# Twelve of 36 weight chunks of the second MoE decoded during the last attention block, in slots that attention no longer uses

## The chip, the cores and the metric

One core of one Trainium2 chip runs the whole program: attention, a first mixture-of-experts layer (MoE) and a second one, in float32 inputs and outputs. The metric is the device time of one execution in microseconds (us), here the median of 3 runs. A core has five engines that work side by side, each through its own instructions in order: TensorE (PE, matmuls; PEld is its weight load), VectorE (DVE), ScalarE (ACT), GpSimd (POOL) and SyncE (SP, which here issues nearly all transfers). They wait for each other by semaphores.

## The reference

```python
def _attn_ref(q, k, v, w1, b1, w2):              # q, k, v: (4, 8, 576, 64)
    scores = scale * np.matmul(q, k.transpose(0, 1, 3, 2))
    ...
    h = np.maximum(x @ w1 + b1, 0.0)             # x: relative positions
    bias = h @ w2
    scores = scores + bias.transpose(2, 0, 1)[None, :, :, :]
    scores = scores - np.max(scores, axis=-1, keepdims=True)
    attn = np.exp(scores)
    attn = attn / (np.sum(attn, axis=-1, keepdims=True) + 1e-09)
    return np.matmul(attn, v).astype(np.float32)

def _moe_ref(x, w_in, w_out, g_ln):              # x: (2304, 512), w_in: (512, 1024)
    h = x @ w_in
    ...
    solu = h * sm                                # sm: softmax of h
    ln = (solu - mu) / np.sqrt(var + 1e-06) * g_ln
    return (ln @ w_out).astype(np.float32)

def _moe2_ref(x, w_gate, w_val, w_out):          # w_gate, w_val: (512, 1536), w_out: (1536, 512)
    gate = 1.0 / (1.0 + np.exp(-(x @ w_gate)))
    val = x @ w_val
    return (gate * val @ w_out).astype(np.float32)
```

The three follow each other: the second MoE reads what the first one wrote for the same tokens.

## The kernel before

**Arithmetic.** Matmuls take float16. Each float32 operand is scaled by a power of two and split into a high and a low float16 half, and a product is three matmuls (high x high, high x low, low x high). The MoE weights come in as 64-bit words, loaded as two 32-bit integers per value.

**A chunk.** A weight chunk is 128 rows by 512 values. The second MoE has 36: 12 each of gate, value and output weights, in column groups jc = 0, 1, 2 of four chunks. Each goes through the same steps:

1. load (L660): SP issues a 512 KB transfer into a raw tile `wraw`;
2. decode (L166 to L176): one step on ScalarE (L171) and three on VectorE (L172, L173, L176) make float32 of the integers, in place in `w2f`;
3. the square's sum on ScalarE (L1087), for the scale;
4. the scale of a column group (`w2_scale`), from sums on TensorE (L147, L1097) and a chain of small VectorE steps; for the output weights one scale for all (`w2_scale_out`, the last of the four; its end is L1112);
5. split (L663 to L669): GpSimd scales (L665), ScalarE writes the high half (L668), GpSimd the low half (L669), again in place.

**Attention.** It runs in 72 ticks, one per (batch pair, query block, head pair, ...). Tick t does the score matmuls (L530), the maximum with the bias added on VectorE (L550), the exponentials on ScalarE (L557); a step later the split of the probabilities (L568 on ScalarE or L566 on VectorE, L569 and L570 on GpSimd) and a transposing transfer by SP (L572); four steps later the PV matmuls (L590). The loop runs steps 0 to 77. K, V and bias live in 24 slots of one tile `gk`: 16 for the K and V of a batch pair by head pair, 8 for biases in rotation. The last block (batches 2 and 3, second query block) is ticks 56 to 71. Its head pairs leave their K and V one after the other, the last PV being that of tick 71.

**The first MoE** fills the gaps: its 18 token tiles are cut into pieces (`moe_items`), of which up to three are issued per step. A tile goes: first product on TensorE (L737), maximum (L748), exponential, normalization and square on VectorE and ScalarE (L756 to L768), scaling on GpSimd (L770, L771: the e step), transposes (L780), halves (L782, L783), second product (L794), and the store of the result x2 by SP (L802). Five or so tiles are left when attention ends.

**The second MoE's weights** are worked on from then on. All pieces stand in one list, `units`: 36 decodes, 3 + 1 scales, 36 splits. `W2A` = 12 are issued when attention is over (L1133), `W2B` = 10 behind each further x2 store (L1139: nothing of them is issued ahead of that store on the issuing engine), the rest among the gate and value products of the first token group (`gate_val`, L1304, with VectorE's steps L1310 and L1172, a pair per 128 columns). Three raw tiles rotate. Behind `w2_scale_out` VectorE forms sums and differences of weight blocks (`w2_sums`, 98 additions with those of the tokens, all at L1190), with which the token groups from the third on are computed by seven products in place of eight (`product`, L1266). The second product of the layer is `second_out` (L1334, 36 matmuls per tile).

**What sets the order.** TensorE follows the program's order inside the attention loop. Elsewhere, and on the other engines, a scheduler orders the instructions by priorities and modelled times; once ordered, every engine works strictly in order, and SP's transfers too.

Line numbers here and in the prediction are those of the kernel before.

Of the kernel before, what the change touches and what calls it, by code (L numbers as in the profile page):

```python
# [91 lines left out]
def attn_moe_kernel(  # L92
# [996 lines left out]
    def w2_split(mat, jc, c):
        split_w(w2f[mat][:, 4 * jc + c], sw[:, jc, S_G + mat:S_G + mat + 1], w2h16[mat][:, 4 * jc + c, 0],  # L1090
                w2h16[mat][:, 4 * jc + c, 1], w2t_p.tile([128, 512], F32, name="w2tmp", tag="w2sgn"))

    def w2_scale(jc):
        pow2(w2st, [(4 * jc, 4 * jc + 4)], sw[:, jc, P_G:P_G + 1], sw[:, jc, S_G:S_G + 1], psx[0], 13)
        tot = (psx[0] or ps_v).tile([128, 512], F32, name="cols", tag="m" if psx[0] else "v")
        for c in range(4):
            pe.matmul(tot, ones16, w2h.pop(("sq", jc, c)), start=(c == 0), stop=(c == 3))  # L1097
        mx = sm0.tile([128, 1], F32, name="colmax", tag="colmax")
        dve.tensor_reduce(out=mx, in_=tot, axis=AX, op=ALU.max)
        root2(mx, 1, sw[:, jc, P_L:P_L + 1], sw[:, jc, S_L:S_L + 1], 13)  # L1100
        dve.scalar_tensor_tensor(out=sw[:, jc, W_CG:W_CG + 1], in0=col(P_F), scalar=2.0 ** -21,
                                 in1=sw[:, jc, P_G:P_G + 1], op0=ALU.mult, op1=ALU.mult)

# [350 lines left out]
```

## Time and profile before

| | us |
|---|---|
| median of 3 runs (lowest, highest) | 1081.53 (1080.61, 1082.23) |
| the profiled execution: its own time | 1084.97 |
| its span, first to last instruction | 1083.2 |
| PE busy (share) | 910.7 (84%) |
| DVE busy (share) | 768.5 (71%) |
| ACT busy (share) | 619.4 (57%) |
| POOL busy (share) | 413.0 (38%) |

The profile is of one execution, and all times in the trace are counted from the start of its span. "Busy" of TensorE is not a pace: matmuls overlap, and their ends are modelled. So its pace is read from a run of like matmuls that follow each other. "Idle before" says how long an engine waited ahead of an instruction and who released it.

### The profile page before, as it was taken

How to read it: one execution, taken by the hardware profiler on the slowest of the kernel's cores; microseconds unless marked ns; L12 is line 12 of the kernel's file. 1: busy time of each engine (PE TensorE's matmuls, PEld its weight loads, DVE VectorE, ACT ScalarE, POOL GpSimd, SP SyncE). 2: the span in 40 equal slices, each digit the busy share in tenths (PEclk: the TensorE clock that was granted, in tenths of full speed). 3: DMA queues.
4: the chain of work that ended last, by engine and by line, in shares of the span. 5: the costliest groups of instructions: out<-in, count | busy, mean ns of one | idle time of the engine just before them, and what ended most of it. 6: DMA issues, size and time to landing. Idle time of an engine off the chain costs nothing. (4 is left out here: it accounts for less than half of the span.)

```text
span 1083.2 us, 24445 instructions
## 1 busy us (share of the span) xinstructions
PE 910.7 (84%) x9806; PEld 652.1 (60%) x9806; DVE 768.5 (71%) x1552; ACT 619.4 (57%) x1283; POOL 413.0 (38%) x370
## 2 busy tenths in 40 slices
PE   2556573768887889989999888896999999999998
PEld 2534453555666667676776656344577866865873
DVE  6879997985566676655755899999973862881760
ACT  4787775767676788776973777744342331331331
POOL 2366555745556555544560377758000000000000
PEclk9756665868999889989999898898999999999999
DMA  7979999899799799998965556501001010001001
GB/s 229 289 240 205 238 229 275 157 232 204 158 191 192 165 200 191 190 211 169 172 124 159 162 156 181 170 20 39 30 18 52 1 55 24 2 1 39 2 1 39
DMA packets 261442, 146.58 MB, mean 135 GB/s; under 512 B 217680, under 2 KB 231504, under 8 KB 261328
## 3 DMA queue, kind: packets, MB, share of 16 engines
q1 hardware_dynamic: 259264, 143.18, 56.2%
q0 software_dynamic: 1536, 1.58, 0.5%
q8 instruction: 77, 1.26, 0.5%
q10 hardware_dynamic: 528, 0.26, 0.1%
q14 instruction: 37, 0.30, 0.1%
HBM read 82.46 MB, written 20.05 MB: 95 GB/s over the span
## 5 line engine op out<-in xcount | busy, mean ns | idle before, releaser
L569 POOL TENSOR_TENSOR p<-p,p 128x1024 f16<-128x1024 f32 x72 | 154.7, 2149 | 150.1 <-ACT p L568 112.9
L1190 DVE TENSOR_TENSOR fr<-prod,fr 128x512 f32<-128x512 f32 x126 | 85.2, 688 | 93.8 <-PE prod L1266 92.1
L1334 PE MATMUL ops<-w2f,gv 128*128 128x512 f16 x648 | 144.2, 381 | 5.3 <-POOL w2f L669 3.9
L794 PE MATMUL x2ps<-lt,w1f 128*128 128x128 f16 x1728 | 114.0, 228 | 18.2 <-DVE lt L783 13.4
L557 ACT ACTIVATE p<-p,m,sc 128x576 f32<-128x576 f32 x144 | 124.0, 862 | 2.7
L794 PEld LDWEIGHTS <-w1f 128*128 128x128 f16 x1728 | 107.6, 103 | 28.6 <-issue 21.1
L550 DVE CUSTOM_DVE_ANT_0 p<-s_ps,gk 128x576 f32<-128x576 f32 x144 | 104.3, 751 | 21.9 <-PE s_ps L530 19.0
L1334 PEld LDWEIGHTS <-gv 128*128 128x128 f16 x648 | 63.6, 98 | 80.6 <-issue 7.4
L1304 PE MATMUL s_ps<-xb,w2f 128*128 128x512 f16 (+1 forms) x576 | 100.1, 332 | 8.8 <-DVE fr L1310 8.5
L590 PE MATMUL xps<-gk,pt 128*128 128x64 f16 (+1 forms) x2240 | 89.2, 203 | 17.8 <-DMA pt<-p 14.9
L590 PEld LDWEIGHTS <-pt 128*128 128x128 f16 (+1 forms) x2240 | 82.9, 107 | 29.1 <-DMA pt<-p 19.1
L530 PE MATMUL s_ps<-gk,qt 64*128 64x288 f16 (+1 forms) x960 | 91.9, 316 | 6.3 <-DVE m L550 3.7
L443 PEld LDWEIGHTS <-mask 128*128 128x128 f16 (+1 forms) x1312 | 60.9, 116 | 58.2 <-issue 24.3
L1266 PEld LDWEIGHTS <-w2f 128*128 128x128 f16 x864 | 84.5, 98 | 11.8 <-issue 1.1
L1304 PEld LDWEIGHTS <-w2f 128*128 128x128 f16 x576 | 56.9, 100 | 50.2 <-issue 14.5
L1171 ACT ACTIVATE gv<-fr 128x512 f16<-128x512 f32 (+1 forms) x60 | 34.7, 584 | 83.5 <-DVE fr L1324 70.5
L737 PE MATMUL hps<-w1f,xt 128*128 128x512 f16 x312 | 76.6, 396 | 0.6 <-DVE qt L282 0.6
L443 PE MATMUL bp<-rhs,mask 128*128 128x64 f16 (+1 forms) x960 | 52.2, 221 | 25.8 <-DVE gb L463 14.6
L555 ACT ACTIVATE m<-m,sc 128x1 f32<-128x1 f32 x144 | 40.6, 286 | 58.0 <-DVE m L550 58.0
L1266 PEld LDWEIGHTS <-w2s 128*128 128x128 f16 x648 | 63.4, 98 | 7.3
L568 ACT ACTIVATE p<-p 128x1152 f16<-128x1152 f32 x54 | 62.6, 1159 | 5.4 <-DMA pt<-p 3.8
L737 PEld LDWEIGHTS <-xt 128*128 128x128 f16 x384 | 36.9, 101 | 46.8 <-issue 12.1
(192 smaller groups left out, 1776.2 us busy)
## 6 DMA issues: line engine op xcount, KB each, us to landing
gk<-bias_d SPq DMA_DIRECT2D x24, 576.0 KB
wraw<-in_moe_w_out_dram SPq DMA_DIRECT2D x20, 512.0 KB
wraw<-in_moe_w_gate_dram SPq DMA_DIRECT2D x12, 512.0 KB
wraw<-in_moe_w_val_dram SPq DMA_DIRECT2D x12, 512.0 KB
sraw<-in_q_dram SPq DMA_DIRECT2D x12, 384.0 KB
sraw<-in_k_dram SPq DMA_DIRECT2D x12, 384.0 KB
sraw<-in_v_dram SPq DMA_DIRECT2D x12, 384.0 KB
bias_d<-gk SPq DMA_DIRECT2D x8, 576.0 KB
```

The source lines that it names most:

```text
L443: pe.matmul(big[0:np_, jj // 8, o:o + 64], lhsT, rhs[i].rearrange("p c h g -> p (c h g)"), start=(i == 0), stop=(i == 1),)
L530: glob["qk"] = pe.matmul(ss[hh][p0:p1, n, 0:288], qt[rows, nr * ql + r, p0:p1], kt[rows, o:o + 288], start=(m == 0), stop=(m == 2))
L550: dve.tensor_tensor_reduce(out=pp[:, hh].rearrange("p (i j) -> p i j", i=2), in0=ss[hh][:, :, 0:288], in1=bi.rearrange("p (i j) -> p i j", ...
L557: act.activation(out=pp[:, hh], in_=pp[:, hh], func=ACTF.Exp, bias=m[:, 2 + hh:3 + hh], scale=col(C), accum_out=sm[:, c + hh:c + hh + 1])
L569: pool.tensor_tensor(out=p16[:, :, 640:1152], in0=pp[:, :, 0:512], in1=hi[:, :, 0:512], op=ALU.subtract)
L590: pe.matmul(o, a, b_, start=(n == 0), stop=(n == len(seq) - 1))
L737: pe.matmul(h, xt[:, xl, kk, off:off + 128], win16[:, 2 * kk + n, wl], start=(kk == 0 and xl == 0 and wl == 0), stop=(kk == 3 and xl == 1),)
L794: pe.matmul(ps[:, dc], wout16[:, f, wl, 128 * dc:128 * dc + 128], lt[:, ll, f], start=(n == 0), stop=(n == 23))
L1190: dve.tensor_tensor(out=out_, in0=a, in1=b, op=op)
L1266: pe.matmul(p[:, jf, 0:nn], w(wl, kk, jf), x(xl, kk), start=(m == 0), stop=(m == 5))
L1304: pe.matmul(ps[:, 0:n], w[:, 4 * (j // 4) + c, wl, o:o + 128], xx[:, 0:n, c, xl, :], start=(m == 0), stop=(m == 11))
L1334: pe.matmul(ps, gvs[j // 4][:, gl, j % 4, 128 * tt:128 * tt + 128], w2h16[2][:, j, wl], start=(m == 0), stop=(m == 35))
```

## The change

Twelve of the 36 decodes move into the last attention block and its end. `AHEAD` lists for each the step of its load, the step of its decode, and the place of the raw words: 0 and 1 are two tiles of a new pool, 8, 10, 12 and 14 are bias slots of `gk` that are no longer read. The load is issued behind the transpose of the tick before (`tc.issue_after`), the decode behind the latest conversion of probabilities on ScalarE (`glob["hi"]`), both without the priority that attention's own work has. The decoded words no longer have tiles of their own (`w2f`): gate and value chunks and six of the output chunks go into `gk` (`gk32`, the same tile in rows of 512), where K, V and biases were, the other six into `w2x`. The squares of the first value chunks go into the raw K and V tile. When attention is over, 29 of the 76 pieces have been issued with `W2A` = 16, in place of 12; the thirteenth piece, the first group's scale, stands at attention's end.

```diff
@@ -47,7 +47,9 @@
+AHEAD = ((60, 63, 0), (61, 64, 1), (65, 67, 0), (66, 68, 1), (67, 69, 8), (69, 71, 10), (70, 72, 0), (70, 73, 1),
+         (71, 74, 8), (72, 75, 10), (73, 76, 12), (74, 76, 14))
-W2A = 12
+W2A = 16
...
+    kvr = kraw_p.tile([128, NKR, 2, 5, D], F32, name="kv")
+    kvraw = [kvr[:, i] for i in range(NKR)]
...
+    W2AT = ((20, 0, 10), (24, 4, 14), (8, 9, 18, 19, 28, 29))
+
+    def w2(mat, j, n=1):
+        if mat == 2:
+            t, a = (gk32, W2AT[2][j]) if j < 6 else (pools["w2x"], j - 6)
+        else:
+            t, a = gk32, W2AT[mat][j // 4] + j % 4
+        return t[:, a] if n == 1 else t[:, a:a + n]
...
+    def w2_early(n, t):
+        mat, jc, c = W2SEQ[n]
+        place = AHEAD[n][2]
+        if place < 2:
+            raw = pools["w2r"].tile([128, 512, 2], I32, name="wraw", tag=f"wraw{place}")
+        else:
+            raw = gk[0][:, place:place + 2].rearrange("p s e -> p (s e)")[:, 0:1024].bitcast(I32) \
+                .rearrange("p (f t) -> p f t", t=2)
+        src, rows, cols = w2_src(mat, jc, c)
+        with tc.issue_after(trs[min(t, nticks) - 1].ins):
+            sp.dma_start(out=raw.rearrange("p f t -> p (f t)"), in_=src[rows, cols].bitcast(I32))
+        early[mat, jc, c] = raw
+
+    def w2_dec(mat, jc, c):
+        raw = early.pop((mat, jc, c), None)
+        if raw is None:
+            raw = load_w(pools["w2r"], *w2_src(mat, jc, c))
+        w = w2(mat, 4 * jc + c)
+        decode(w, raw, pool if c < W2P else dve)
...
@@ -1052,7 +1152,20 @@
                 a_pv(t - LAG_PV)
             if 0 <= t - LAG_PV - LAG_X < nticks:
                 a_xt(t - LAG_PV - LAG_X)
+        if t == AHEAD[0][0]:
+            ahead = ExitStack()
+            pools["w2r"] = enter(ahead, "w2e", 1)
+        for n, (t0, t1, _) in enumerate(AHEAD):
+            if t == t1:
+                with tc.issue_after(glob["hi"].ins):
+                    units.pop(0)()
+        for n, (t0, t1, _) in enumerate(AHEAD):
+            if t == t0:
+                w2_early(n, t)
     in_order.close()
+    while len(units) > 76 - 13:
+        units.pop(0)()
+    ahead.close()
     att.close()
...
-    w2r_p = enter(d2, "w2r", 3, "right")
-    w2d_p = enter(d2, "w2d", 1, "right")
-    w2f = [w2_p.tile([128, 12, 512], F32, name=f"w2f{i}") for i in range(3)]
+    pools["w2r"] = enter(d2, "w2r", 3, "right")
+    pools["w2d"] = enter(d2, "w2d", 1, "right")
+    pools["w2x"] = w2_p.tile([128, 6, 512], F32, name="w2x")
```

How the order changes is seen in three places. On SP, from the last transposes of attention on, the order before is this (x_d is the store of x2, xb its load for the second MoE, wraw a chunk's raw words):

```order
L572 DMA_TRANSPOSE pt<-p_9418 128x18x128
L572 DMA_TRANSPOSE pt<-p_9527 128x18x128
L802 DMA x_d<-x_9581 128x1024
L572 DMA_TRANSPOSE pt<-p_9620 128x18x128
L1153 DMA xb<-x_d 128x4x1024
L802 DMA x_d<-x_9870 128x1024
L660 DMA wraw<-in_moe_w_gate_dram 128x1024 x4
L660 DMA wraw<-in_moe_w_val_dram 128x1024 x4
L660 DMA wraw<-in_moe_w_gate_dram 128x1024
```

After the change, whose early loads are at its line 1062 and whose other lines are up to two further down than before, from the same transposes on:

```order
L574 DMA_TRANSPOSE pt<-p_9571 128x18x128
L804 DMA x_d<-x_9625 128x1024
L1062 DMA gk<-in_moe_w_gate_dram 128x1024
L574 DMA_TRANSPOSE pt<-p_9670 128x18x128
L1062 DMA gk<-in_moe_w_gate_dram 128x1024 x3
L1205 DMA xb<-x_d 128x4x1024
L804 DMA x_d<-x_9938 128x1024
L662 DMA wraw<-in_moe_w_val_dram 128x1024 x4
L662 DMA wraw<-in_moe_w_gate_dram 128x1024 x4
L804 DMA x_d<-x_10315 128x1024
L662 DMA wraw<-in_moe_w_val_dram 128x1024
L804 DMA x_d<-x_10541 128x1024
```

Eight more loads of this kind stand ahead of these rows, between the transposes; behind the last row come the fifteen loads that are left. On ScalarE, around the conversion of tick 66 (the x2 tiles are x, the chunk's words gk or wraw), the order before is:

```order
L557 ACTIVATE p,sums<-p,m,sc 128x576 x2
L568 ACTIVATE p_9100<-p 128x2x576
L767 ACTIVATE hs,mm<-e,mm 128x1024
L555 ACTIVATE m<-m,sc 128x1
L557 ACTIVATE p,sums<-p,m,sc 128x576
L555 ACTIVATE m<-m,sc 128x1
L281 ACTIVATE qt<-qtp,sc 128x256
L557 ACTIVATE p,sums<-p,m,sc 128x576
```

And after it (L173 is the decode's step, L1077 the square's sum, L559 the exponential, L570 the conversion):

```order
L559 ACTIVATE p,sums<-p,m,sc 128x576 x2
L570 ACTIVATE p_9123<-p 128x2x576
L173 ACTIVATE gk<-wraw 128x512
L769 ACTIVATE hs,mm<-e,mm 128x1024
L557 ACTIVATE m<-m,sc 128x1
L559 ACTIVATE p,sums<-p,m,sc 128x576
L283 ACTIVATE qt<-qtp,sc 128x256
L557 ACTIVATE m<-m,sc 128x1
L559 ACTIVATE p,sums<-p,m,sc 128x576
L1077 ACTIVATE kv,w2st<-gk 128x512
```

The third decode's first step stands directly behind the conversion of tick 66, ahead of tick 67's exponentials, and its square's sum behind them. On GpSimd, when attention's last split is done, the order before has three e steps (mm, e) between the last probabilities and the first split of a chunk:

```order
L570 TENSOR_TENSOR p_9620<-p,p_9620 128x2x64
L770 TENSOR_TENSOR mm<-mm,nhalf 128x1
L771 TENSOR_SCALAR e<-e,mm 128x1024
L770 TENSOR_TENSOR mm<-mm,nhalf 128x1
L771 TENSOR_SCALAR e<-e,mm 128x1024
L770 TENSOR_TENSOR mm<-mm,nhalf 128x1
L771 TENSOR_SCALAR e<-e,mm 128x1024
L665 TENSOR_SCALAR w2tmp<-w2f_9972,sw 128x512 x2
```

After it:

```order
L572 TENSOR_TENSOR p_9670<-p,p_9670 128x2x64
L772 TENSOR_TENSOR mm<-mm,nhalf 128x1
L773 TENSOR_SCALAR e<-e,mm 128x1024
L667 TENSOR_SCALAR w2tmp<-gk,sw 128x512 x2
L671 TENSOR_TENSOR gk<-w2tmp,gk 128x512 x2
L667 TENSOR_SCALAR w2tmp<-gk,sw 128x512 x2
L671 TENSOR_TENSOR gk<-w2tmp,gk 128x512 x2
L667 TENSOR_SCALAR w2tmp<-gk,sw 128x512 x2
L671 TENSOR_TENSOR gk<-w2tmp,gk 128x512 x2
L772 TENSOR_TENSOR mm<-mm,nhalf 128x1
```

One e step stands ahead of the first split in place of three behind the last probabilities, and six splits ahead of the next. On TensorE the rows are too many to show; in the order before, 213 gate and value matmuls of 512 columns stand ahead of the matmul of the last scale (tot, three columns) and 75 behind it, in the order after 143 and 145. Ahead of the last block the orders of all engines are the same but for single instructions.

## Rows read from the trace of the kernel before

**Rows 1.** Stages: start:end, length, busy per engine (count), granted clock, DMA share, GB/s.

```profile
503.00:563.00 60.00, 58.42 (x887) 45.04 (x885) 39.73 (x106) 49.86 (x108) 31.78 (x27) 1.00 0.77 143
563.00:582.40 19.40, 19.40 (x290) 14.66 (x288) 6.71 (x19) 8.24 (x17) 6.80 (x8) 1.00 0.66 145
582.40:717.00 134.60, 114.06 (x856) 69.72 (x853) 121.25 (x250) 89.48 (x184) 71.46 (x56) 0.91 0.50 157
717.00:820.90 103.90, 93.79 (x564) 55.44 (x563) 86.75 (x130) 40.56 (x77) 36.87 (x24) 0.97 0.10 34
820.90:1083.20 262.30, 258.45 (x1944) 190.12 (x1943) 143.74 (x226) 70.67 (x110) 0.00 (x0) 1.00 0.05 18
```

**Rows 2.** TensorE's time line, then the chain that ended last: start, length, what, count.

```profile
593.05 5.34 PE L737 MATMUL s_ps<-w1f,xt 128*128 128x512 f16 x24 [0.31 <-DVE mm L748]
598.23 5.47 PE L794 MATMUL x2ps<-lt,w1f 128*128 128x128 f16 x95
639.09 1.04 PE L780 MATMUL ltp<-id_sb,e 128*128 128x128 f32 x8
...
798.25 5.40 PE s_ps L1304 x48
820.89 55.18 PE prod L1266 x504
876.07 15.54 PE ops L1334 x72
```

**Rows 3.** VectorE's groups, 582.4 to 717: count, busy us, mean ns, idle before.

```profile
L173 DVE SCALAR_TENSOR_TENSOR w2f<-wraw,w2f 128x512 int32<-128x512 int32 x36 | 32.7, 909 | 0.3
L176 DVE SCALAR_TENSOR_TENSOR w2f<-wraw,w2f 128x512 int32<-128x512 int32 x36 | 28.5, 793 | 0.1
L172 DVE TENSOR_SCALAR w2f<-w2f 128x512 int32<-128x512 int32 x36 | 22.5, 626 | 5.2 <-ACT w2f L171 4.8
L1172 DVE TENSOR_TENSOR gv<-fr,gv 128x512 f16<-128x512 f32 x8 | 7.7, 967 | 0.7 <-ACT gv L1171 0.7
L1310 DVE SCALAR_TENSOR_TENSOR fr<-s_ps,fr 128x512 f32<-128x512 f32 x9 | 6.1, 682 | 0.8 <-ACT fr L1309 0.8
```

**Rows 4.** VectorE's time line: a decode's steps, and the end of the last scale.

```profile
588.94 0.43 DVE L172 TENSOR_SCALAR w2f<-w2f 128x512 int32<-128x512 int32 x1 [0.85 <-ACT w2f L171]
589.40 0.69 DVE L173 SCALAR_TENSOR_TENSOR w2f<-wraw,w2f 128x512 int32<-128x512 int32 x1
...
696.49 1.65 DVE L173 SCALAR_TENSOR_TENSOR w2f<-wraw,w2f 128x512 int32<-128x512 int32 x1
716.91 0.15 DVE L1112 SCALAR_TENSOR_TENSOR sc<-sc 128x1 f32<-128x1 f32 x1
```

**Rows 5.** SP's time line: the store of the third tile after attention.

```profile
629.58 0.33 SPq L802 DMA_DIRECT2D x_d<-x  x1
```

**Rows 6.** GpSimd's time line: its first instruction after attention.

```profile
609.12 0.78 POOL L770 TENSOR_TENSOR mm<-mm,nhalf 128x1 f32<-128x1 f32 x1 [30.79 <-DVE mm L763]
```

**Rows 7.** ScalarE's groups: the maximum's wait (503 to 567), and a decode's steps.

```profile
L555 ACT ACTIVATE m<-m,sc 128x1 f32<-128x1 f32 x24 | 6.8, 285 | 5.6 <-DVE m L550 5.6
...
L171 ACT ACTIVATE w2f<-wraw 128x512 f32<-128x512 f32 x36 | 24.2, 671 | 22.1 <-DMA wraw<-in_moe_w_gate_dram 8.8 <-DMA wraw<-in_moe_w_val_dram 7.9 <-DMA wraw<-in_moe_w_out_dram 5.2
L1087 ACT ACTIVATE w2junk<-w2f 128x512 bf16<-128x512 f32 x24 | 14.9, 623 | 5.8 <-DVE w2f L176 5.3 <-DVE sw L156 0.3 <-DVE acc L145 0.2
L1087 ACT ACTIVATION_READ_ACCUMULATOR w2junk<-w2f 128x1 f32 x24 | 4.5, 187 | 0.0
```

**Rows 8.** Time lines of SP, ScalarE and TensorE at the end of attention.

```profile
531.47 3.18 SPq L572 DMA_TRANSPOSE pt<-p  x1
538.62 1.16 ACT L568 ACTIVATE p<-p 128x1152 f16<-128x1152 f32 x1
568.89 2.67 SPq L572 DMA_TRANSPOSE pt<-p  x1
581.50 0.98 PE L590 MATMUL xps<-gk,pt 128*128 128x64 f16 x28
```

**Rows 9.** Chain that ended last: a chunk landing; and SP's issues (ns min/median/max).

```profile
629.96 4.73 DMA wraw<-in_moe_w_val_dram
...
L660 SPq DMA_DIRECT2D wraw<-in_moe_w_gate_dram x12: 327/328/1069, 583.4 to 649.1; - x12
```

More of the change, by code (lines that the diff above doesn't have):

```diff
@@ new lines, in w2_scale @@
+    def w2_scale(jc):
+        pow2(w2st, [(4 * jc, 4 * jc + 4)], sw[:, jc, P_G:P_G + 1], sw[:, jc, S_G:S_G + 1], psx[0], 13)
+        tot = (psx[0] or ps_v).tile([128, 512], F32, name="cols", tag="m" if psx[0] else "v")
+        for c in range(4):
+            pe.matmul(tot, ones16, w2h.pop(("sq", jc, c)), start=(c == 0), stop=(c == 3))
+        mx = sm0.tile([128, 1], F32, name="colmax", tag="colmax")
+        dve.tensor_reduce(out=mx, in_=tot, axis=AX, op=ALU.max)
+        root2(mx, 1, sw[:, jc, P_L:P_L + 1], sw[:, jc, S_L:S_L + 1], 13)
+        dve.scalar_tensor_tensor(out=sw[:, jc, W_CG:W_CG + 1], in0=col(P_F), scalar=2.0 ** -21,
+                                 in1=sw[:, jc, P_G:P_G + 1], op0=ALU.mult, op1=ALU.mult)
@@ new lines, in w2_scale_out @@
+    def w2_scale_out():
+        pow2(w2st, [(24 + 4 * jc, 28 + 4 * jc) for jc in range(3)], sw[:, :, P_O], None, psx[0])
+        dve.tensor_tensor(out=sw[:, :, W_M], in0=sw[:, :, P_O], in1=sw[:, :, P_L], op=ALU.mult)
+        dve.tensor_reduce(out=col(CO), in_=sw[:, :, W_M], axis=AX, op=ALU.max)
+        dve.reciprocal(col(RM), col(CO))
+        for jc in range(3):
+            dve.scalar_tensor_tensor(out=sw[:, jc, S_O:S_O + 1], in0=sw[:, jc, P_L:P_L + 1], scalar=2.0 ** 14,
+                                     in1=col(RM), op0=ALU.mult, op1=ALU.mult)
+        glob["so"] = dve.scalar_tensor_tensor(out=col(CO), in0=col(CO), scalar=2.0 ** -21, in1=col(P_F), op0=ALU.mult, op1=ALU.mult)
@@ new lines, in urgent @@
+    def urgent(f):
+        with tc.high_priority(W2PRIO):
+            f()
+    W2SEQ = [(m, jc, c) for jc in range(3) for m in range(2) for c in range(4)]
+    decs = [(lambda m=m, jc=jc, c=c: w2_dec(m, jc, c)) for jc in range(3) for m in range(2) for c in range(4)]
+    decs += [(lambda jc=jc, c=c: w2_dec(2, jc, c)) for jc in range(3) for c in range(4)]
+    units = decs[:8]
+    for jc in range(3):
+        units += decs[8 * jc + 8:8 * jc + 12]
+        units += [lambda jc=jc: w2_scale(jc)]
+        units += [lambda m=m, jc=jc, c=c: w2_split(m, jc, c) for m in range(2) for c in range(4)]
+        units += decs[8 * jc + 12:8 * jc + 16 if jc < 2 else None]
@@ L1019, in attn_moe_kernel @@
+    units += [lambda: urgent(w2_scale_out)]
+    units += [lambda jc=jc, c=c: w2_split(2, jc, c) for jc in range(3) for c in range(4)]
     in_order = ExitStack()
@@ L1089, in w2_split @@
[L1089 to L1102, printed above, removed]
@@ L1126, in attn_moe_kernel @@
-    units += [lambda: urgent(w2_scale_out)]
-    units += [lambda jc=jc, c=c: w2_split(2, jc, c) for jc in range(3) for c in range(4)]
-    psx = [None]
+    pools["w2r"] = enter(d2, "w2r", 3, "right")
+    pools["w2d"] = enter(d2, "w2d", 1, "right")
+    pools["w2x"] = w2_p.tile([128, 6, 512], F32, name="w2x")
     glob["tail"] = None
@@ L1297, in gate_val @@
             both = ps_s.tile([128, 2, 4, 128], F32, name="s_ps", tag="s_ps")
-            for i, w in enumerate(w2h16[:2]):
+            for i in range(2):
                 ps = both[:, i]
```

81 lines of the change are left out of this document (34 added, 47 removed).

## The prediction

> **What bounds the kernel now.** I read the table of stages first, then the groups of instructions of the stretch that the change empties, then the time lines of the queues on either side. The stages [rows 1] show where time can be had at all. From 820.9 us to the end TensorE is busy for 258.45 of 262.30 us in products that nothing here touches. The last attention block keeps it busy too: 58.42 of 60 us in 503 to 563, at the full clock, with ScalarE at 49.86 and VectorE at 39.73. Between the last PV matmuls (582.4) and the first product (820.9 [rows 2]) lie 238.5 us in which TensorE is not fed: VectorE is busy for 121.25 of 134.60 us up to 717, where the last scale of the second MoE (w2_scale_out) is done [rows 4], and for 86.75 of 103.90 us behind it. The granted clock is 0.91 in the first part, so TensorE is there for a while at the lower of its two levels (1.2 GHz).
>
> How much it could gain follows from its own paces [rows 2]: 0.2225 us for a matmul of 512 columns (5.34/24), 0.058 us for one of the first MoE's second product (5.47/95), 0.13 for a transpose (1.04/8), 0.1125 for a gate matmul of 256 columns (5.40/48), 0.216 for one of the output (15.54/72). In the order before, there stand ahead of the last scale's matmul 79 of hps, 480 of x2ps, 213 of gate and value, 40 transposes and 12 column sums: 17.6 + 27.6 + 47.4 + 5.2 + 2.7 = 100.5 us. Behind it stand 75 of 512 columns, 288 of 256 and 216 of the output: 16.7 + 32.4 + 46.7 = 95.8 us. Together 196 of 238.5 us; some 42 us is all that a perfect feed could give back.
>
> **The change part by part.**
>
> *Decodes that leave the stretch.* The 36 decodes cost VectorE 32.7 + 28.5 + 22.5 = 83.7 us there [rows 3], 2.33 each; twelve of them go into the attention block and its end. At the mean that removes 28.0 us. The first twelve, though, ran with GpSimd idle and took 0.43 + 0.69 + 0.69 = 1.8 us each (the third step is like the second) [rows 4], so that the 24 left may all be slow ones, and the removal only 21.6. I take the middle, 24.8; 21.6 and 28.0 are the bounds.
>
> The rows show what makes a decode slow: with GpSimd idle its second step takes 0.69 us, beside a split 1.65 us [rows 4]. The Trainium skill (SBUF — State Buffer, Who interferes with whom) says why, and speaks against part of the gain: a VectorE instruction with two inputs in SBUF and a GpSimd one that reads SBUF exclude each other, and the later one waits to the end of the other. By that rule the waiting belongs to GpSimd's 36 splits, which all stay, and the removal is at its lower bound: the sum below would come to 1075 in place of 1072. The two durations agree with the rule; where the waits go no row shows.
>
> *Gate work that moves behind the last scale.* In the order after, 143 gate and value matmuls stand ahead of it in place of 213, and VectorE has 6 pairs of gate steps ahead of it in place of 9: three pairs less at 0.68 + 0.97 [rows 3], 5.0 us. VectorE's work up to the scale is then 121.25 - 24.8 - 5.0 = 91.5 us. With the idle time of before (134.60 - 121.25 = 13.4) the scale would be done at 582.4 + 91.5 + 13.4 = 687.3.
>
> *Loads behind stores.* SP issues in order, and the loads of the remaining chunks stand behind the stores of first-MoE tiles: eight behind the first store after attention, one behind the second, fifteen behind the third, which in the trace goes out at 629.58 [rows 5]. Before, 23 stood behind that store, and the scale was done 87.4 us later. Eight decodes (18.6) and three pairs (5.0) less make it 63.8, so 693.4. This is the later of the two estimates and the one I take. The store can come later too, since 20 gate matmuls that wait for splits now stand ahead of that tile in TensorE's order; that they wait two splits more is my upper bound, 10 us with the e step between them (703.4).
>
> *GpSimd.* It idles 30.79 us up to 609 [rows 6]. Its splits can now begin when attention ends, but six stand ahead of the next tile's e step. I cost this at nothing, because that step waited until 609 before as well; if that cover is gone, tile and third store are late (the 10 us above).
>
> *The attention block.* Five decodes stand on ScalarE and VectorE ahead of the last softmax; the other seven lie in 563 to 582 and just behind, where VectorE is busy for 6.71 and ScalarE for 8.24 of 19.4 us [rows 1]. On ScalarE one is 0.67 + 0.62 + 0.19 = 1.48 us [rows 7], 7.4 for the five, against 10.1 us of idle time in 503 to 563. That time is not free at will: 5.6 us of it are waits for VectorE's maximum [rows 7]. PV matmuls come late after their transposes, the last is issued at 568.89 and used at 581.50 [rows 8], so a delay of several us on ScalarE reaches GpSimd and SP but not TensorE. What it can reach is the first MoE's chain, which has no such lag. Issuing is cheap: a load takes SP 0.33 us, twelve 4 us [rows 9]. I take +2 us; the lower bound is 0 (all hidden), the upper 14.7 (the third rival).
>
> *Behind the scale.* TensorE now has 145 x 0.2225 + 32.4 + 46.7 = 111.4 us of matmuls there, 15.6 more than before. Before, it lost 103.9 - 95.8 = 8.1 us to waits. VectorE has the 98 additions of the weight sums as before and three more pairs among them, so the waits don't vanish, but more of the matmuls hang on no addition. I take 4.6, between 0 and 8.1: 116 us.
>
> **Sum.** 582.4 + 2 + 111.0 (to 693.4) + 116 = 811.4 for the first product, against 820.9: 9.5 us less, and nothing changes behind it. The profiled execution took 1084.97 us (a span of 1083.2 and 1.8 around it), so its like would take 1075.5. The median of the runs shown is 1081.53, 3.4 less than that execution; taken off the median, I predict 1072.
>
> **Rivals.**
>
> *The full removal* (chance 0.27). The stores come on time, the scale is done at 687.3, attention hides everything, and TensorE finds its matmuls ready (111.4): 798.7, so 22.2 us less, 1059. For it: TensorE has 42 us of slack in the stretch, and VectorE is the engine that is full. Against it: fifteen loads hang on one store.
>
> *Handed back behind the scale* (chance 0.10). The third store comes 10 us late, the scale at 703.4, and TensorE then works off its 111.4 us with all 8.1 us of waits: 822.9 and 2.0 us more, 1083.5, at the edge of no change. For it: 70 gate matmuls, 15.6 us, went from a part where TensorE has time to one where it has little. Against it: while TensorE waits ahead of the scale, those matmuls could run early only if splits were done, and these come sooner now.
>
> *The loads come late in the attention block, and the kernel is slower* (chance 0.18). ScalarE and VectorE work in order, so a decode whose chunk has not landed holds up the softmax behind it. A chunk took 4.73 us to land when attention was over [rows 9]. The third load stands behind the transpose of tick 64, issued at 531.47 and taking 3.18, and its decode directly behind tick 66's conversion, 538.62 + 1.16: 5.1 us [rows 8]; the next two have the same distance of two ticks. The DMA share in 503 to 563 is already 0.77 [rows 1]. If a chunk takes 10 us there, three decodes wait 4.9 us each, 14.7 us, and nothing hides it from the first MoE's chain: 582.4 + 14.7 + 111.0 + 116 = 824.1, 3.2 slower, 1085; from some 9 us a chunk on the gain is gone. Against it: at 4.73 us a chunk all three are there in time.
>
> The Trainium skill (DMA: Bandwidth & Descriptors, Queues, rings and completion order) speaks for that last case: what SP issues goes through one ring on each DMA engine and is taken up in order, so chunks and transposes queue behind each other. No row here shows a chunk in flight with a transpose.
>
> That the change doesn't do what it says needs no case: the orders show the twelve loads, and five decodes ahead of the last softmax.
>
> **How the numbers follow.** The forecast has 0.45, the full removal 0.27, handed back 0.10, slower 0.18. About 0.2% (2.2 us) is what a measurement of this kernel can tell from no change. Faster by more: 0.45 + 0.27 = 0.72; of the handed-back cases 0.08 lie within it and 0.02 beyond: slower 0.20. The forecast's own range is 1062 to 1080 (the removal at 21.6 to 28.0, attention at 0 to 5, waits at 0 to 8.1). The range takes in most of the outer cases: 1057 to 1086.
>
> **What would show it.** Right: 24 decodes in VectorE's groups after the last PV and some 59 us in them; w2_scale_out done near 695; the first product near 811; the last PV within 4 us of 582.4. The full removal: products from 800 on. Handed back: the scale beyond 700 and TensorE full behind it. Late loads: ScalarE's decode step waiting for a chunk inside 510 to 565, and a last PV beyond 590. I would be wrong in kind if anything moved ahead of 500 us or behind the first product.

## The result and the profile after

| | before | after |
|---|---|---|
| median of 4 runs (us) | 1081.07 (1077.77 to 1082.23) | 1096.63 (1092.26 to 1098.21) |
| ratio after : before, 95% interval | | 1.0143 (1.0106 to 1.0179) |
| the profiled execution: its own time, its span | 1084.97, 1083.2 | 1092.26, 1090.5 |

The kernel is 1.4% slower; 0.9% faster was forecast. The profiled execution after the change is the fastest of its four, that of before is above its median, so the spans differ by 7.3 us where the medians differ by 15.6. Most of that gap of 8.3 us lies ahead of tick 60, where the order is nearly the same: there the execution after the change is 6.4 us ahead (e1 below, in the order of before throughout, is 5.7 ahead: chance). So two lengths are compared here: **A**, from tick 60's maximum to the end of the last PV matmul, and **B**, from there to the first product, cut at the end of the last scale into B1 and B2. Tick 60's maximum, with which A starts, and tick 71's, the last, on VectorE before the change:

```profile
502.75 0.76 DVE L550 CUSTOM_DVE_ANT_0 p<-s_ps,gk 128x576 f32<-128x576 f32 x1 [0.33 <-PE s_ps L530]
560.23 0.76 DVE L550 CUSTOM_DVE_ANT_0 p<-s_ps,gk 128x576 f32<-128x576 f32 x1
```

And after it, where the kernel's lines are two higher:

```profile
496.39 0.75 DVE L552 CUSTOM_DVE_ANT_0 p<-s_ps,gk 128x576 f32<-128x576 f32 x1
565.68 0.76 DVE L552 CUSTOM_DVE_ANT_0 p<-s_ps,gk 128x576 f32<-128x576 f32 x1
```

The stages after the change (columns as in [rows 1]; the first two cover A but for 0.2 us, the next two are B1 and B2):

```profile
496.60:567.80 71.20, 62.27 (x876) 47.51 (x874) 55.28 (x122) 56.14 (x125) 34.91 (x28) 0.93 0.86 179
567.80:592.20 24.40, 20.78 (x300) 15.04 (x297) 18.27 (x41) 16.00 (x36) 9.30 (x8) 1.00 0.93 250
592.20:708.00 115.80, 96.44 (x779) 60.78 (x778) 96.83 (x206) 73.68 (x144) 65.21 (x57) 0.90 0.39 128
708.00:828.20 120.20, 109.15 (x640) 62.67 (x638) 91.30 (x135) 44.94 (x82) 36.83 (x24) 0.99 0.09 29
828.20:1090.50 262.30, 258.43 (x1944) 190.07 (x1943) 143.69 (x226) 70.75 (x110) 0.00 (x0) 1.00 0.05 18
```

Against [rows 1]: the first stage, the softmax of the last ticks, takes 71.2 us in place of 60.0, with VectorE (the third busy column) busy for 55.28 in place of 39.73 us, and TensorE's clock at 0.93 in place of 1.00. The end of attention takes 24.4 in place of 19.4. (The two tables are not cut at quite the same event. Cut at the start of tick 71's maximum, the parts of A are 69.3 in place of 57.5 us and 26.5 in place of 22.3.) B1 is 115.8 in place of 134.6, B2 is 120.2 in place of 103.9, and the products behind take 262.3 in both. So A costs 16.1 us (95.8 against 79.7), B1 gives back 18.8 and B2 takes 16.4 of them. On TensorE's time line the ends of A and B2, where before [rows 8] and [rows 2] stand:

```profile
591.25 0.98 PE L592 MATMUL xps<-gk,pt 128*128 128x64 f16 x28
...
828.17 1.47 PE L1318 MATMUL prod<-xb,gk 128*128 128x256 f16 x12 [0.78 <-ACT ob L1390]
```

**A.** VectorE and then GpSimd, at the third early decode (L174 is the decode's first VectorE step, L552 the maximum, L571 the split of the probabilities):

```profile
537.11 1.90 DVE L174 TENSOR_SCALAR gk<-gk 128x512 int32<-128x512 int32 x1 [1.70 <-ACT gk L173]
538.93 0.74 DVE L552 CUSTOM_DVE_ANT_0 p<-s_ps,gk 128x576 f32<-128x576 f32 x1
```

```profile
536.60 2.13 POOL L571 TENSOR_TENSOR p<-p,p 128x1024 f16<-128x1024 f32 x1 [3.67 <-ACT p L570]
```

The step that took 0.43 us with GpSimd idle [rows 4] takes 1.90, and ends at 539.01, 0.28 us behind the split's end at 538.73. The next tick's maximum stands behind it. The first four early decodes all show this (first steps of 1.90, 1.95, 1.90 and 1.90, each ending 0.28 or 0.29 us behind a split's end), since ScalarE's conversion, behind which the decode is ordered, is also what releases the split. The fifth, whose first step starts 1.1 us into a split, takes 1.29 and ends 0.28 us behind it too. The fifteen VectorE steps of the five decodes add up to 15.9 us. The Trainium skill (SBUF — State Buffer, Who interferes with whom) says that a tensor_scalar on VectorE can run in a mode that takes the ports shared with GpSimd, and that whichever of the two starts first holds them for its whole instruction; the five ends agree. TensorE's waits in A, first after the change and then before it:

```profile
PE ltp L782 <- DVE xt L656: 3.7, 1, 3.7
PE x2ps L796 <- DVE lt L785: 3.3, 1, 3.3
PE s_ps L739 <- ACT xt L655: 2.3, 2, 1.3
PE ltp L782 <- DVE mm L750: 1.3, 1, 1.3
```

```profile
PE x2ps L794 <- DVE lt L783: 1.6, 1, 1.6
```

With three smaller ones (0.7, 0.6, 0.5) TensorE waits 12.4 us in place of 1.6. Nearly all of it is for the first MoE's chain and the halves of attention's tokens, which stand behind VectorE's and ScalarE's decode steps; none is for a transposed probability. Behind the two longest waits its granted clock is lower:

```profile
533.00:537.00 4.00, 3.87 (x60) 3.52 (x61) 2.41 (x7) 3.92 (x10) 0.41 (x1) 0.67 1.01 228
556.00:561.00 5.00, 4.55 (x49) 3.62 (x50) 3.27 (x8) 4.44 (x11) 0.00 (x0) 0.50 0.81 189
```

0.50 is the level of 1.2 GHz. On the time line, behind the wait of 3.29 us, the 28 matmuls of a PV take 1.70 us in place of 0.98 [rows 8]:

```profile
533.13 1.66 PE L796 MATMUL x2ps<-lt,w1f 128*128 128x128 f16 x24 [3.29 <-DVE lt L785]
534.59 1.70 PE L592 MATMUL xps<-gk,pt 128*128 128x64 f16 x28
```

The 10.8 us of added waits and the slower work of these stretches (an estimate from the two granted clocks: 4 x 0.33 + 5 x 0.50 = 3.8 us) are 14.6 of the 16.1 us.

Behind the last softmax ScalarE waits for chunks, 4.4 us in all with two more rows of 1.36 and 0.37:

```profile
572.80 0.67 ACT L173 ACTIVATE gk<-wraw 128x512 f32<-128x512 f32 x1 [1.22 <-DMA wraw<-in_moe_w_val_dram]
579.94 0.67 ACT L173 ACTIVATE gk<-gk 128x512 f32<-128x512 f32 x1 [1.42 <-DMA gk<-in_moe_w_gate_dram]
```

Ahead of it there is no such wait: the first six chunks were there.

**B.** VectorE's groups in B1 (as in [rows 3]; with the two left out, L174 and L175 of w2x at 4.4 and 4.8 us, they are 24 decodes and 59.3 us), then the end of the last scale, then the stores of SP:

```profile
L175 DVE SCALAR_TENSOR_TENSOR gk<-wraw,gk 128x512 int32<-128x512 int32 x18 | 16.4, 912 | 0.2
L178 DVE SCALAR_TENSOR_TENSOR gk<-wraw,gk 128x512 int32<-128x512 int32 x18 | 15.9, 885 | 0.1
L174 DVE TENSOR_SCALAR gk<-gk 128x512 int32<-128x512 int32 x18 | 12.8, 710 | 1.2 <-ACT gk L173 0.9
...
L178 DVE SCALAR_TENSOR_TENSOR w2x<-wraw,w2x 128x512 int32<-128x512 int32 x6 | 5.0, 828 | 0.1
```

```profile
707.84 0.15 DVE L1102 SCALAR_TENSOR_TENSOR sc<-sc 128x1 f32<-128x1 f32 x1
```

```profile
623.52 0.33 SPq L804 DMA_DIRECT2D x_d<-x  x1
...
644.00 0.33 SPq L804 DMA_DIRECT2D x_d<-x  x1
```

These answer to [rows 4] and [rows 5]. The last scale is done 64.0 us behind the third store (644.00); 63.8 was forecast. In B2 TensorE has 111.4 us of matmuls by the paces of [rows 2], which leaves 8.8 of the 120.2 for waits. The view of waits has 11.1 us, since TensorE is busy for 109.15 us there, and nearly all of them are for VectorE:

```profile
PE s_ps L1356 <- DVE fr L1362: 10.3, 3, 4.8
PE prod L1318 <- ACT ob L1390: 0.8, 1, 0.8
```

Counted in this way, [rows 1] has 10.1 us of waits before the change (103.90 less 93.79). So B2 grew by TensorE's work, 15.4 us of the 16.4.

### The profile page after: what moved, and what is told of

Same layout as the page of the kernel before. It is cut to its first block, busy times and chain, and to the rows that moved or that the text cites. A ratio compares the mean times of both kernels' runs of the same rounds, so it can differ in the third digit from the quotient of the medians.

```text
span 1090.5 us, 24427 instructions
## 1 busy us (share of the span) xinstructions
PE 909.6 (83%) x9806; PEld 647.9 (59%) x9806; DVE 776.7 (71%) x1552; ACT 622.8 (57%) x1285; POOL 409.1 (38%) x370
## 5 line engine op out<-in xcount | busy, mean ns | idle before, releaser
L571 POOL TENSOR_TENSOR p<-p,p 128x1024 f16<-128x1024 f32 x72 | 154.7, 2149 | 148.2 <-ACT p L570 107.7
L559 ACT ACTIVATE p<-p,m,sc 128x576 f32<-128x576 f32 x144 | 124.0, 862 | 2.5
L796 PE MATMUL x2ps<-lt,w1f 128*128 128x128 f16 x1728 | 108.4, 224 | 18.3 <-DVE lt L785 12.9
L796 PEld LDWEIGHTS <-w1f 128*128 128x128 f16 x1728 | 102.5, 100 | 26.8 <-issue 16.5
L1356 PE MATMUL s_ps<-xb,gk 128*128 128x512 f16 (+1 forms) x576 | 103.6, 339 | 16.7 <-DVE fr L1362 14.6
L552 DVE CUSTOM_DVE_ANT_0 p<-s_ps,gk 128x576 f32<-128x576 f32 x144 | 104.1, 750 | 18.5 <-PE s_ps L532 16.0
L1356 PEld LDWEIGHTS <-gk 128*128 128x128 f16 x576 | 57.8, 101 | 59.3 <-issue 26.7
L1318 PEld LDWEIGHTS <-gk 128*128 128x128 f16 x864 | 84.5, 98 | 11.8 <-issue 1.1
L1386 PE MATMUL ops<-gk,gv 128*128 128x512 f16 x324 | 75.2, 379 | 0.0
L445 PE MATMUL bp<-rhs,mask 128*128 128x64 f16 (+1 forms) x960 | 51.3, 218 | 27.4 <-DVE gb L465 16.8
L1386 PE MATMUL ops<-w2x,gv 128*128 128x512 f16 x324 | 73.9, 379 | 0.0
```

Of the source, the lines that this page charges most:

```text
L445: pe.matmul(big[0:np_, jj // 8, o:o + 64], lhsT, rhs[i].rearrange("p c h g -> p (c h g)"), start=(i == 0), stop=(i == 1),)
L552: dve.tensor_tensor_reduce(out=pp[:, hh].rearrange("p (i j) -> p i j", i=2), in0=ss[hh][:, :, 0:288], in1=bi.rearrange("p (i j) -> p i j", ...
L559: act.activation(out=pp[:, hh], in_=pp[:, hh], func=ACTF.Exp, bias=m[:, 2 + hh:3 + hh], scale=col(C), accum_out=sm[:, c + hh:c + hh + 1])
L571: pool.tensor_tensor(out=p16[:, :, 640:1152], in0=pp[:, :, 0:512], in1=hi[:, :, 0:512], op=ALU.subtract)
L796: pe.matmul(ps[:, dc], wout16[:, f, wl, 128 * dc:128 * dc + 128], lt[:, ll, f], start=(n == 0), stop=(n == 23))
L1318: pe.matmul(p[:, jf, 0:nn], w(wl, kk, jf), x(xl, kk), start=(m == 0), stop=(m == 5))
```

## The experiments

All times in us, each run against the kernel before on the same chip; A, B1, B2 from one profiled execution. Three of the orders are that of the kernel before up to the loads (before, e1, e4): their A and B2 agree within 0.03, their B1 lies between 133.2 and 136.8, so that B1 carries some 2 us of chance either way. With early decodes A carries chance too: the changed kernel and e5 have the same order on VectorE, ScalarE, GpSimd and SP throughout A, and their A is 95.8 and 97.4, with the whole difference behind the last softmax. In the rows of e7 and e9 line numbers are one lower than in the changed kernel.

| run | A | B1 | B2 | median | ratio to before (95%) |
|---|---|---|---|---|---|
| before | 79.7 | 134.6 | 103.8 | 1081.07 | |
| after | 95.8 | 115.8 | 120.2 | 1096.63 | 1.0143 (1.0106 to 1.0179) |
| e1_place | 79.7 | 133.2 | 103.8 | 1080.25 | 0.9989 (0.9970 to 1.0008) |
| e2_nodve | 90.1 | 110.2 | 122.0 | 1086.55 | 1.0061 (1.0040 to 1.0082) |
| e3_max | 89.1 | 117.0 | 118.8 | 1088.50 | 1.0051 (1.0026 to 1.0076) |
| e4_loads | 79.7 | 136.8 | 103.8 | 1081.24 | 0.9992 (0.9967 to 1.0017) |
| e5_w2b6 | 97.4 | 122.2 | 104.1 | 1086.13 | 1.0051 (1.0028 to 1.0074) |
| e6_earlier | 94.2 | 112.0 | 122.0 | 1090.53 | 1.0092 (1.0058 to 1.0127) |
| e7_late4 | 84.1 | 123.7 | 106.2 | 1077.53 | 0.9958 (0.9934 to 0.9983) |
| e8_late8 | 84.1 | 129.4 | 103.5 | 1079.52 | 0.9983 (0.9963 to 1.0002) |
| e9_four | 79.7 | 128.7 | 104.4 | 1075.02 | 0.9932 (0.9907 to 0.9957) |
| e10_max_w2b6 | 89.8 | 123.0 | 104.4 | 1080.25 | 0.9974 (0.9953 to 0.9995) |
| e11_four_w2b10 | 79.5 | 125.8 | 106.3 | 1075.86 | 0.9934 (0.9911 to 0.9958) |

### What costs A

**e1_place**, the storage alone:

```diff
-W2A = 16
+W2A = 12
...
-                with tc.issue_after(glob["hi"].ins):
-                    units.pop(0)()
...
-                w2_early(n, t)
...
-    while len(units) > 76 - 13:
-        units.pop(0)()
...
```

> The changed storage alone: decoded words in the K, V and bias tile and in the six-chunk tile, no early load, no early decode, 12 pieces when attention is over; the order of every engine is that of the kernel before. Two lengths are compared in all runs: A, from tick 60's maximum to the end of the last PV matmul (before 79.7 us, after 95.8), and B, from there to the first product (before 238.4, after 235.9). Theory (the early decodes' VectorE steps cost A, and what B gains ahead of the last scale is handed back behind it): A 79.7 and B 238.4 within 1 us each, total 1081 within 2. Rival (the places themselves cost, as the first-step reads and writes in the shared tile): B some us longer, total above 1084.

A and B2 are those of before to the tenth, the time is the same: the places cost nothing.

**e4_loads**, the early loads alone:

```diff
-W2A = 16
+W2A = 12
...
-                with tc.issue_after(glob["hi"].ins):
-                    units.pop(0)()
...
-    while len(units) > 76 - 13:
-        units.pop(0)()
     ahead.close()
+    early.clear()
```

> The storage of the changed kernel with the order of the kernel before, and the twelve early loads added as they stand in the changed one, but read by nobody (each chunk is loaded again after attention). Theory: A 80 to 82, B 238.4 within 1, total 1081 to 1084. Rival (the loads' traffic slows the transposes and K, V and bias transfers of the last block): A 86 or more, total 1088 or more.

A is 79.7. Its stage, to be held against the 0.77 and 0.66 of [rows 1], which make 0.74 over A:

```profile
502.00:581.70 79.70, 78.14 (x1179) 59.95 (x1176) 46.74 (x125) 58.07 (x124) 38.76 (x34) 1.00 1.01 222
```

The transfers are denser (a share of 1.01, 222 GB/s) and TensorE's work ends as before. The loads' traffic is not the cause. Nor do loads that wait for a place hold up the transposes on SP: in the changed kernel's view of waits SP waits ahead of none of the twelve.

**e2_nodve**, the early decodes without VectorE's steps:

```diff
+        ahead_now = [raw is not None]
...
-        decode(w, raw, pool if c < W2P else dve)
+        if ahead_now[0]:
+            act.activation(out=w, in_=raw[:, :, 1].bitcast(F32), func=ACTF.Copy, scale=2.0 ** -5)
+        else:
+            decode(w, raw, pool if c < W2P else dve)
```

> The changed kernel, with the three VectorE steps of the twelve early decodes left out (ScalarE's step and the square stay, and the loads; the words are then other numbers). Theory (VectorE's steps hold up the softmax): A falls from 95.8 to 80 to 84, B stays 236 within 2, total about 1083. Rival 1 (the loads, or ScalarE's two steps, cost A): A stays at 92 to 96, total about 1094. Rival 2 (B is bound by what VectorE still has to do): B falls too, total below 1078.

None of the three came out whole. Up to tick 71's maximum the loss falls from 11.8 us (69.3 against 57.5) to 3.4 (60.9): VectorE's steps are most of that, ScalarE's the rest. But A is still 90.1, because behind the softmax ScalarE is now earlier and the chunks are not. ScalarE (L1072 is its one step left of a decode) and then TensorE:

```profile
569.95 0.69 ACT L1072 ACTIVATE gk<-wraw 128x512 f32<-128x512 f32 x1 [1.96 <-DMA wraw<-in_moe_w_val_dram]
...
574.87 0.66 ACT L1072 ACTIVATE gk<-gk 128x512 f32<-128x512 f32 x1 [3.00 <-DMA gk<-in_moe_w_gate_dram]
```

```profile
577.82 4.33 PE L739 MATMUL s_ps<-w1f,xt 128*128 128x512 f16 x11 [5.28 <-ACT xt L655]
581.99 4.18 PE L796 MATMUL x2ps<-lt,w1f 128*128 128x128 f16 x72
586.01 0.98 PE L592 MATMUL xps<-gk,pt 128*128 128x64 f16 x28
```

The halves (xt) queue on ScalarE behind the decode that waits for its chunk, TensorE stands 5.28 us for them, and the last PVs stand behind that on TensorE. B is 232.2, 3.7 shorter, but that says nothing of VectorE there: the steps left out stood in A, B1 has its 24 decodes as in the changed kernel (58.7 us of VectorE, against 59.3), and the scheduler made another order, with 135 gate and value matmuls ahead of the last scale in place of 143.

**e3_max**, VectorE's steps behind the maximum:

```diff
-            dve.tensor_tensor_reduce(
+            glob["mx"] = dve.tensor_tensor_reduce(
...
-                with tc.issue_after(glob["hi"].ins):
+                with tc.issue_after(glob["hi"].ins), tc.issue_after(glob["mx"].ins):
```

> The changed kernel, with each early decode's VectorE steps ordered behind the maximum of the tick that is then current, so that the first step no longer meets GpSimd's split of the probabilities. Theory of the shared port (a first step of 0.43 us takes 1.9 beside the split and holds the next maximum): first steps at 0.43 to 0.7, A 88 to 91, total about 1091. Rival (it is VectorE's work in itself, 1.8 us a decode ahead of the softmax, wherever it stands): A 94 to 97, total about 1096.

A falls by 6.7, 4.6 of them up to tick 71's maximum. Three of the five first steps became short, as this one; the first two met a split all the same (1.88 and 1.97):

```profile
542.46 0.42 DVE L174 TENSOR_SCALAR gk<-gk 128x512 int32<-128x512 int32 x1
```

What is left there, 7.2 us for five decodes, I put down to their own time on VectorE and ScalarE and to those two; this was not tested further.

**e6_earlier**, three later loads sooner:

```diff
-AHEAD = ((60, 63, 0), (61, 64, 1), (65, 67, 0), (66, 68, 1), (67, 69, 8), (69, 71, 10), (70, 72, 0), (70, 73, 1),
-         (71, 74, 8), (72, 75, 10), (73, 76, 12), (74, 76, 14))
+AHEAD = ((60, 63, 0), (61, 64, 1), (65, 67, 0), (66, 68, 1), (67, 69, 8), (69, 71, 10), (68, 72, 0), (69, 73, 1),
+         (70, 74, 8), (72, 75, 10), (73, 76, 12), (74, 76, 14))
```

> The changed kernel with three of the later loads issued one or two steps sooner (chunks 7, 8 and 9 behind the transposes of ticks 67, 68 and 69 in place of 69, 69 and 70). Theory (what A loses behind the last softmax, 26.5 us to the last PV against 22.3 before, is ScalarE waiting 4.4 us for chunks with the halves of attention's tokens queued behind): ScalarE's waits for chunks between the last softmax and the last PV fall below 2 us, A 92 to 93.5, total about 1093. Rival (the decode's own steps fill that stretch): A 95 to 96, total 1096. Second rival (SP stands ahead of a transpose waiting for a place): A above 96.

ScalarE's waits for chunks between the last softmax and the last PV, in the view of waits:

```profile
ACT kv L1077 <- DVE gk L178: 5.0, 4, 3.4
ACT gk L173 <- DMA gk<-in_moe_w_gate_dram: 0.8, 2, 0.6
```

Those for chunks fall from 4.4 to 0.8 us, but A by 1.7 only: the squares there wait 5.0 for VectorE in place of 3.9. And 1.7 is hardly more than the 1.6 by which A differs between the changed kernel and e5, and in e6 ScalarE's order around the halves is another too. So what late chunks cost A is not shown.

### What takes back B1's gain

**e5_w2b6**, one number:

```diff
-W2B = 10
+W2B = 6
```

> The changed kernel with W2B = 6 in place of 10: fewer pieces behind each store, so that 214 gate and value matmuls stand ahead of the last scale on TensorE and 74 behind it, as before the change (213 and 75; the changed kernel has 143 and 145). B is split at the last scale: B1 from the last PV to w2_scale_out (before 134.6, changed 115.8), B2 from there to the first product (103.8, 120.2). Theory (B2 grew because TensorE got those matmuls behind the scale, where it is the bound): B2 104 to 106, B1 118 to 126, A still 95.8 within 1, total 1083 to 1092. Rival (B2 is set by something else, as VectorE's additions): B2 stays above 116, total 1096 or more.

The 71 matmuls that went back ahead of the scale are 71 x 0.2225 = 15.8 us, and B2 falls by 16.1, to the length of before:

```profile
718.20:822.20 104.00, 94.63 (x567) 56.50 (x565) 86.69 (x129) 40.36 (x76) 36.30 (x24) 0.97 0.10 34
```

B1 grows by 6.4 only. The median is 10.5 lower with nothing done for A, which was expected to stay within 1 of 95.8 and is 97.4. B2 goes with the number of gate and value matmuls behind the last scale in every run: 103.5 to 104.4 with 74 or 75 of them, 106.2 and 106.3 with 81 and 82 (e7, e11), 118.8 and 120.2 with 145 (e3 and the changed kernel), 122.0 with 153 (e2, e6).

### Both put right

**e7_late4** and **e8_late8**, only decodes that no softmax follows:

```diff
+AHEAD = ((66, 72, 0), (67, 72, 1), (67, 73, 8), (69, 73, 10))
+W2A = 12
+W2B = 9
...
-    while len(units) > 76 - 13:
+    while len(units) > 76 - 4:
```

```diff
+AHEAD = ((66, 72, 0), (67, 72, 1), (67, 73, 8), (69, 73, 10), (72, 99, 0), (72, 99, 1), (73, 99, 12), (74, 99, 14))
+W2A = 12
+W2B = 8
...
+            glob["xt"] = act.activation(out=xt[:, 0, hp], in_=xtp[:, o:o + w], func=ACTF.Copy)
...
-    while len(units) > 76 - 13:
-        units.pop(0)()
+    with tc.issue_after(glob["xt"].ins):
+        while len(units) > 76 - 8:
+            units.pop(0)()
```

> Only four decodes ahead, all of them behind the last softmax, with loads three to six steps sooner; W2A = 12, W2B = 9, so that 207 gate and value matmuls stand ahead of the last scale. Theory (a decode is free where no softmax is behind it and its chunk is there; and what B1 gains stays gained where the matmuls stay ahead): A 79.7 to 81.5, B1 126 to 131, B2 104 to 106, total 1075 to 1079. Rival 1 (anything in the attention block costs): A above 84, total 1081 or more. Rival 2 (B is set by the stores that the loads stand behind): B1 133 or more, total 1081.

> Eight chunks loaded in the attention block (four three to six steps sooner, four behind the last transpose); four decoded behind the last softmax, four right behind attention's last halves on ScalarE; W2A = 12, W2B = 8, so that 214 gate and value matmuls stand ahead of the last scale. Theory: A 79.7 to 82, B1 118 to 126, B2 104 to 106, total 1067 to 1075. Rival 1 (the block is disturbed all the same): A above 84. Rival 2 (B1 is set by stores and loads and not by VectorE's decodes): B1 130 or more, total 1077 or more.

A is 84.1 in both, above what both expected, though up to tick 71's maximum it is 57.45 as before. All 4.4 us come behind it. On ScalarE in e7:

```profile
572.41 0.63 ACT L1076 ACTIVATE kv<-gk 128x512 bf16<-128x512 f32 x1 [3.84 <-DVE gk L177]
...
573.80 0.36 ACT L654 ACTIVATE xt<-xtp 128x256 f16<-128x256 f32 x1
```

The square waits 3.84 us for VectorE's decode, and attention's halves queue behind it; the chunks were there. VectorE holds up the first MoE as well. The same maximum of that chain, before and then in e7, whose tick 60 starts within 0.02 us of the one before:

```profile
568.88 0.69 DVE L748 CUSTOM_DVE_ANT_0 hs<-hps,zero 128x512 f32<-128x512 f32 x1 [1.67 <-PE hps L737]
```

```profile
573.58 0.68 DVE L749 CUSTOM_DVE_ANT_0 hs<-hps,zero 128x512 f32<-128x512 f32 x1
```

It stands 4.7 us later, behind the decode's steps. Eight chunks gain less in B1 (129.4) than four (123.7): the third store comes 54.2 us behind the last PV, where in e7 it is 45.6. In e8 the last four chunks are decoded behind attention, and W2B is 8 in place of 9. Which of the two costs that was not separated.

**e9_four**, the same four behind the halves:

```diff
+AHEAD = ((66, 75, 0), (67, 75, 1), (67, 75, 8), (69, 75, 10))
...
+            glob["xt"] = act.activation(out=xt[:, 0, hp], in_=xtp[:, o:o + w], func=ACTF.Copy)
...
-                with tc.issue_after(glob["hi"].ins):
+                with tc.issue_after(glob["xt"].ins):
```

(What else e7 has against the changed kernel stays.)

> The four early decodes of the run before this (e7_late4: A 84.1, B1 123.7, B2 106.2, total 1077.5 against 1081.6), with their ScalarE step ordered behind the halves of attention's tokens that it held up; the loads stand where they stood; 214 matmuls ahead of the last scale. Theory (A was longer because ScalarE's squares waited 3.84 us for VectorE with those halves queued behind): A 79.7 to 81, B1 123 to 127, B2 104 to 106, total 1073 to 1076. Rival (VectorE's steps in that stretch hold the first MoE's maximum and halves wherever they stand): A 83 to 85, total 1077 to 1079.

A is 79.71. The halves and then the decode on ScalarE, and VectorE's four first steps, 1.42 us together with GpSimd idle:

```profile
569.44 0.39 ACT L654 ACTIVATE xt<-xtp 128x256 f16<-128x256 f32 x1
569.71 1.24 ACT L172 ACTIVATE gk<-wraw 128x512 f32<-128x512 f32 x2
...
576.11 0.63 ACT L1076 ACTIVATE kv<-gk 128x512 bf16<-128x512 f32 x1 [2.90 <-DVE gk L177]
```

```profile
571.58 1.42 DVE L173 TENSOR_SCALAR gk<-gk 128x512 int32<-128x512 int32 x4
```

The square waits 2.90 us again, with nothing of attention behind it. This beats both kernels, by 0.7% the one before. It is thereby shown that A was longer in e7 by the place of the decodes ahead of the halves. VectorE's steps moved behind the first MoE's maximum with them, so how much each engine's queue cost was not separated. B1, 128.7, is above the 123 to 127 expected.

**e10_max_w2b6**, all twelve with both remedies:

```diff
-W2B = 10
+W2B = 6
...
-            dve.tensor_tensor_reduce(
+            glob["mx"] = dve.tensor_tensor_reduce(
...
-                with tc.issue_after(glob["hi"].ins):
+                with tc.issue_after(glob["hi"].ins), tc.issue_after(glob["mx"].ins):
```

> All twelve early decodes, with both remedies at once: VectorE's steps behind the maximum (A 89.1 alone, from 95.8) and W2B = 6 (B 226.3 alone, from 235.9). Theory (the two causes are separate and add): A 88 to 91, B 225 to 228, total 1078 to 1083, so no slower than the kernel before. Rival (the second remedy takes from the same loss as the first): total 1085 or more.

A is 89.8 and B 227.3; each remedy alone gave 89.1 and 226.3. The causes are separate. Twelve early decodes are then 0.3% faster than none.

**e11_four_w2b10**, e9 with one number changed:

```diff
-W2B = 9
+W2B = 10
```

> As the run with four decodes behind the halves, with W2B = 10 in place of 9: 206 gate and value matmuls ahead of the last scale, 82 behind it. Theory: A the same, B1 1 to 3 us shorter, B2 1 to 2 us longer, total within 2 us of that run. Rival (the stores set B1): B1 unchanged, total 1 to 2 us longer.

B1 is 2.9 shorter, B2 1.9 longer, the time within 1 us of e9. B2 follows the eight matmuls that went behind the scale (1.8 us by their pace); the gain in B1 is within what B1 varies by chance.

## Why the prediction was wrong

**The attention block: the step that failed.** It took "+2 us" from ScalarE's 1.48 us a decode and its idle time, on the ground that a delay "reaches GpSimd and SP but not TensorE". It measured 16.1, beyond the upper bound of 14.7. The ground held for what it was said of: TensorE waits for no transposed probability in A. But VectorE's part was not priced at all: three steps a decode, ahead of the maximum on an engine that works in order, and the first of them behind GpSimd's split of the same conversion. Of the 11.8 us up to tick 71's maximum the loads alone are 0.0 (e4), ScalarE's steps with them 3.4 (e2), VectorE's steps the other 8.4, of which a better place gives back 4.6 (e3). The sentence on the first MoE's chain, which has no lag, was the right one and should have carried the term: TensorE was busy for 58.42 of 60 us [rows 1], so that it had next to no idle time in which to take up a delay of that chain.

**The port.** I set GpSimd's hold against the 36 weight splits alone and for steps with two inputs. In the block it is the one-input first step that waits, for the probabilities' split.

**The late loads.** The rival had the wrong place: ahead of the last softmax no chunk was late. That the kernel came out slower, as this rival has it, is luck: its mechanism had no part in it. Behind the last softmax ScalarE waited 4.4 us, with the halves queued behind; e6, with less of that, has A 1.7 shorter, hardly more than it varies by chance. The Trainium skill (DMA: Bandwidth & Descriptors, Queues, rings and completion order) spoke for that rival, with one ring on each DMA engine that takes up what SP issues in order; in e4 none of it reaches A. How the 4.3 us that A lost there divide among late chunks, ScalarE's squares and VectorE's steps is open; e7 and e9 show that four decodes ahead of the halves cost as much with their chunks there.

**The removal.** 24 decodes and 59.3 us: right ("some 59"). But the 24.8 us taken for it never entered the sum, which went by the stores: at the lower bound the eight decodes there would be 14.4 us and not 18.6, which makes 1076 where I wrote 1075. And the top of my range by its own terms is 1081.7, not 1080. The way from the third store to the scale: 64.0 against 63.8. The store itself came 51.8 us behind the last PV in place of 47.1; 4.7 of the 10 that I set as a bound, and the delay is there at the second store already (31.3 behind the last PV, where before it was 26.5). B1 was to be 111.0 and is 115.8: these 4.7 us. It is more than chance: the third store comes 51.3 to 54.2 us behind the last PV in the six runs with twelve early decodes, 46.2 to 49.5 in the three of the order before. What makes it late was not separated; GpSimd's splits ahead of the e step and the 20 matmuls that I named both stand there.

**Behind the scale.** 111.4 us of matmuls, right, as e5 shows from the other side. The waits were 8.8 in place of 4.6, above the bound of 8.1, where I had expected them to fall because more matmuls hang on no addition; they did not. With that, the handing back, which I held for a case of 0.10 tied to a late store, needs no late store: it was in my own sum (12.1 of the gain before the scale), and I took B1's gain for larger than it was. B fell by 2.5 us, where 11.5 was in the sum (238.5 to 227).

**Sizes.** By A and B the change is 13.6 us slower, where 9.5 faster was forecast. Of these 23.1 us 14.1 are A (16.1 for 2), 4.8 B1 (115.8 for 111.0) and 4.2 B2 (120.2 for 116).

## What to carry to other kernels

Where work is moved into the middle of a pipeline, price it on every engine that it touches, in order with what queues behind it, and look at what its own trigger releases at the same moment on an engine that it can collide with (here GpSimd's split). Idle time behind the last consumer was free here (e9), and idle time between two links of a chain was not. When a critical chain is shortened, count what the order moves to the far side of its end: if another engine is the bound there, the gain can go back (here 16.4 of 18.8 us), and the number that sets the order can be worth as much as the work removed (e5).

## What the runs showed of the hardware

A one-input VectorE step of 0.43 us (32-bit integers, SBUF to SBUF) that starts beside a GpSimd instruction ends 0.28 or 0.29 us behind that one's end, in all seven cases after the change and all four of e3, GpSimd's instruction being the split of 2.13 us each time. The maximum, which reads PSUM, keeps its time beside the same split: 45 of them lie wholly inside one after the change, at 0.74 to 0.76 us. And beside a 128x1 instruction of GpSimd, recorded at 2.47 us, the step kept its 0.42 us (after the change, at 588.46). Six MB of loads more in the block (a DMA share of 1.01 in place of 0.74 over A, e4) moved no matmul's end in A by more than 0.03 us.
